# A new order of 880 tasks, with new engines and buffers, for a fused RWKV-5 and MLP-mixer kernel

## The chip, the cores and the metric

The kernel runs on one core of a Trainium2 chip. The metric is the device time of one execution in microseconds (us), the median over several runs. Five engines work side by side, each through its own queue in program order: PE (matrix products; its weight loads, PEld, overlap them), DVE, ACT and POOL (element-wise work), and SP (here only a queue of DMA issues). Sixteen DMA engines move data. Products write to PSUM, 8 banks of 2 KB per partition; DVE and ACT empty the banks.

## The reference, cut to what matters

Inputs r, k, v are (4, 8, 768, 48) in f32: 4 batches, 8 heads, 768 steps, 48 channels. The first half is a linear recurrence over the steps, the second half a mixer block on its output x of (4, 768, 384):

```python
for t in range(S):
    kt, vt, rt = (k[:, :, t], v[:, :, t], r[:, :, t])
    cur = np.einsum('bhd,bhe->bhde', u[None] * kt, vt)
    y[:, :, t] = np.einsum('bhd,bhde->bhe', rt, state + cur)
    state = w[None, :, :, None] * state + np.einsum('bhd,bhe->bhde', kt, vt)
...
xt = x.transpose(0, 2, 1)
h = np.maximum(xt @ w_tok1, 0.0) @ w_tok2       # over the 768 steps, 256 wide inside
u = x + h.transpose(0, 2, 1)
h2 = np.maximum(u @ w_ch1, 0.0) @ w_ch2         # over the 384 channels, 1536 wide inside
return (u + h2).astype(np.float32)
```

## The kernel before, in words

**Tiling.** The 768 steps of a batch are 6 chunks of 128. For a chunk, k and r are multiplied by tables of powers of the decay (on DVE or POOL; tile `kr`, tables `wnat`, `wp`, and `wnpair`, `wpair` where two chunks are loaded as one window `win`), turned so that channels lie on partitions (on PE with a copy out of PSUM into `rka`/`rkb`, or with a DMA transpose into `rk`), and multiplied with each other into scores (`at_ps`). DVE masks the scores into `AT` (kind `mul512p`), PE weighs v by them into `y_ps`, adds what comes from the state, and the result is copied to `x_b`. A step's product with itself (the u term) goes by `pr`, `ad_ps`, `adg`, `yd`. The state `S` is carried from chunk to chunk through `kv_ps`.

The mixer of a batch then makes `h1` from `x_b` and `wtok1` (kinds hid6, or hid3, hid2, hid1 for batch 0, which takes the chunks as they come), goes back over the steps with `wtok2` (kind back), and turns u so that channels lie on partitions: for batch 0 and half of batch 1 on PE (kind turn_x, tile `hx_ps`), for the rest by a DMA transpose `uT<-u_sb` (kind turn_u). Twelve products up (kind up, `z_ps`, three matmuls of 384 columns each) and the products down (kind down, `h_ps`) follow for each half of the batch.

**Whole and half products.** Most matmuls use all 128 rows of the PE array. Those that contract over 64 rows use half of it: scores (kinds scj, sc, sc2: two heads side by side, each on 64 rows), and, for batch 0, whose chunks go in pairs, everything that contracts over the 64 steps of a half window: yv (v weighed), addp2 (own term added), kvp and the second part of kvp_id (state).

**The order.** Nothing in the kernel decides the order when it runs. Every piece of work is a task (a number, an engine, a kind, a function that issues it and its dependences); lists at the head of the file, made by a planner offline, give all the rest:
- `ORDER` (line 21): the sequence in which the 880 tasks are issued. Each engine's queue is what falls to it in this sequence, and the engine keeps to it. So a wait at the head of a queue holds all behind it.
- `BUFS`: for each pool of buffers (`m` are the PSUM banks, 7 of them), which buffer each new tile takes in turn. A task that takes a buffer waits for the last reader of what lay in it.
- `ENGINES`: for each task that can go to either of two or three engines, which one.
- `FILL` (line 139): before which product tasks zero products are issued, and how many. They multiply a tile of zeros and keep PE busy.
- `WAITS`: loads that wait for other loads (not changed).

```python
def run(self):
    done = set()
    for n in self.order:
        emit, deps = self.tasks[n]
        self.now = n
        emit()
        done.add(n)
...
def fill(bank, fresh):
    for i in range(FILL.get(plan.now, 0)):
        pe.matmul(bank, warm[:, 0:128], warm[:, 0:bank.shape[-1]], start=fresh, stop=True, skip_group_check=True)
```

Thirteen more zero products of 512 columns are tasks of their own (867 to 879, kind warm); `FILL[879]` doubles the last.

All instructions issued through these queues have the line number 239 in the profile, so groups are told apart by tile names.

**Task numbers that the text uses.** Batch 0 works on three windows of two chunks. Its tasks:

| what | window 0 | window 1 | window 2 |
|---|---|---|---|
| loads k, r, v (SP) | 51, 52, 53 | 54, 55, 56 | 57, 58, 59 |
| scaled k, two halves | 120, 121 | 149, 150 | 179, 180 |
| scaled r, two halves | 118, 119 | 147, 148 | 177, 178 |
| turned on PE: k, r (tr_all) | 123, 122 | 152, 151 | 182, 181 |
| copied out: k, r | 124, 125 | 153, 154 | 183, 184 |
| product k by r (prod2), summed (sm2), copied (copy_ad) | 126, 127, 128 | 155, 156, 157 | 185, 186, 187 |
| scores, two halves (scj) | 132, 135 | 161, 164 | 191, 194 |
| masks (DVE) | 133, 134, 136, 137 | 162, 163, 165, 166 | 192, 193, 195, 196 |
| v cast; own terms | 129; 130, 131 | 158; 159, 160 | 188; 189, 190 |
| v weighed (yv), own added (addp2) | 138, 139 | 167, 168 | 197, 198 |
| state products, state kept | 140, 143; 141, 144 | 169, 173; 170, 174 | 199; 200 |
| from the state (ys) | 145 | 171, 175 | 201, 203 |

23 is the first product (`w_ps`, the decay spread over partitions), 24 its logarithm (`lnw`), 27 to 30 the four tables (`wnpair`, `wpair`), 8 and 10 the index tables on POOL (`iota_i`), 9 and 11 their casts on DVE. 205, 206, 207 are hid3, hid2, hid1 of batch 0. 111 is the load of `wtok1`, issued by POOL. 518, 547, 576 are the scores of the chunk pairs of batch 2, 698, 727, 756 those of batch 3.

Of the kernel before, what the change touches and what calls it, by code (L numbers as in the profile page):

```python
# [62 lines left out]
    0, 1, 2, 3, 4, 5, 0, 1, 2, 3, 5, 4, 0, 1, 3, 2, 5, 4, 0, 1, 3, 5, 4, 2,  # L63
    ],
# [8 lines left out]
    ],  # L73
    'kp': [
    0, 1, 2, 3, 4, 5, 1, 3, 4, 0, 2, 5, 3, 2, 1, 4, 5, 2, 1, 3, 0, 5, 4, 1, 3, 2, 0,
# [63 lines left out]
FILL = {132: 3, 140: 3, 206: 1, 879: 1}  # L139
# [1116 lines left out]
```

## Time and profile before

| | |
|---|---|
| median of 3 runs | 160.15 us (160.04 to 160.2) |
| profiled execution: span from first to last instruction | 158.2 us |
| profiled execution: its whole time | not given; runs less span: 1.95 us |
| PE busy | 151.8 us (96%) |
| DVE, POOL, ACT busy | 107.0, 90.1, 77.7 us |
| bytes moved by DMA | 27.39 MB, 173 GB/s in the mean |
| granted PE clock, mean | 0.998 |

PE's busy time counts a product from its start to the end of its pipeline, so products that follow closely overlap: a busy PE isn't a PE at its peak. What counts for PE's pace is the distance from one start to the next. In a timeline row the columns are start, length, engine, line, operation, tiles (out<-in), shape and count, and in brackets how long the engine was idle before and what ended that. In a row of windows they are the stretch, its length, and then for each engine its busy time and its number of instructions, the granted PE clock, the mean busy share of the DMA engines (over 1 where transfers overlap) and GB/s. A DMA row on SPq or POOLq shows the issue, not the transfer.

### The profile page before, as it was taken

To read this page: it belongs to the slowest core of one execution; us is meant where nothing else is said; L and a number is where in the kernel's file an instruction comes from. 1 tells how busy PE (TensorE), PEld (TensorE's weight loads), DVE (VectorE), ACT (ScalarE), POOL (GpSimd) and SP (SyncE) were. 2 spreads that over 40 slices of the span, in tenths; PEclk is the share of its full clock that TensorE was granted. 3 is DMA by queue.
4 is the path that set the end of the run, shared out by engine and by line. 5 is a ranking of instruction groups with operands and counts; after the bars stand their busy time and mean duration, and the time that the engine had idled before them with its cause. 6 is when DMAs were issued, how large, how long until landed. Compare 5 with 4: busy or idle time off the path is not lost.

```text
span 158.2 us, 4001 instructions
## 1 busy us (share of the span) xinstructions
PE 151.8 (96%) x1574; PEld 101.3 (64%) x1574; DVE 107.0 (68%) x218; ACT 77.7 (49%) x187; POOL 90.1 (57%) x120
## 2 busy tenths in 40 slices
PE   6988999999999999999999999999999999999991
PEld 1356767776767676666677665576666566666660
DVE  2689992468967994467989637898987465432071
ACT  3677797737990581478476440235643102463000
POOL 7859969444183799999928999398920000000000
PEclk9999999999999999999999999999999999999999
DMA  4999999999989999999999989999992075300044
GB/s 125 265 261 264 205 204 210 229 204 210 227 176 187 203 230 195 187 210 136 220 194 173 227 158 129 190 193 215 145 274 101 29 176 146 126 0 4 0 151 147
DMA packets 88148, 27.39 MB, mean 173 GB/s; under 512 B 82753, under 2 KB 87234, under 8 KB 88130
## 3 DMA queue, kind: packets, MB, share of 16 engines
q1 hardware_dynamic: 85776, 23.86, 76.1%
q0 software_dynamic: 2160, 3.15, 11.7%
q8 instruction: 12, 0.20, 0.5%
q10 hardware_dynamic: 194, 0.14, 0.3%
q14 instruction: 6, 0.05, 0.1%
HBM read 20.65 MB, written 4.72 MB: 160 GB/s over the span
## 4 chain that ended last, share of the span: by engine, by line
PE 87%; DVE 4%; DMA 3%; POOL 2%; ACT 1%; issue 1%; POOLq 0%; ACTq 0%
PE h_ps L239 35%; PE z_ps L239 29%; PE y_ps L239 6%; PE at_ps L239 4%; PE kv_ps L239 3%; PE hT_ps L239 3%; PE hx_ps L239 3%; DVE kr L239 3%; DMA uT<-u_sb 3%; PE tr_ps L239 2%; PE ad_ps L239 1%; PE trk L239 1%; POOL mask L239 1%; ACT rka L239 1%; POOL bm L239 1%
## 5 line engine op out<-in xcount | busy, mean ns | idle before, releaser
L239 PE MATMUL h_ps<-wch,zr 128*128 128x384 bf16 (+2 forms) x300 | 53.4, 319 | 0.0
L239 PE MATMUL z_ps<-uT,wch 128*128 128x384 bf16 x288 | 52.4, 327 | 0.3 <-DMA uT<-u_sb 0.3
L239 ACT ACTIVATE zr<-z_ps 128x384 bf16<-128x384 f32 x63 | 28.7, 492 | 36.1 <-PE z_ps L239 35.9
L239 PEld LDWEIGHTS <-wch 128*128 128x128 bf16 x288 | 31.1, 114 | 13.4 <-DMA uT<-u_sb 0.7
L239 PEld LDWEIGHTS <-zr 128*128 128x128 bf16 x300 | 27.6, 98 | 15.7
L239 DVE TENSOR_TENSOR AT<-at_ps,mask 128x512 bf16<-128x512 f32 x48 | 30.6, 682 | 2.2 <-PE at_ps L239 2.2
L239 DVE TENSOR_SCALAR zr<-z_ps 128x384 bf16<-128x384 f32 x33 | 17.7, 554 | 13.5 <-PE z_ps L239 13.5
L239 POOL TENSOR_TENSOR yd<-vb,adg 128x384 f32<-128x384 bf16 x13 | 10.6, 829 | 10.8 <-ACT vb L239 5.9
L239 DVE TENSOR_TENSOR osb<-u_sb,h_ps 128x384 f32<-128x384 bf16 (+2 forms) x19 | 10.0, 531 | 9.6 <-PE h_ps L239 9.0
L239 PEld LDWEIGHTS <-kr 128*128 128x128 bf16 (+1 forms) x196 | 11.6, 97 | 3.9 <-DVE kr L239 0.7
L239 POOL TENSOR_TENSOR kr<-rt,wp 128x384 bf16<-128x384 f32 x12 | 12.0, 1005 | 3.1 <-DMA rt<-in_r_dram 3.1
L239 POOL TENSOR_TENSOR ku<-kw,u_bc 128x384 f32<-128x384 f32 x12 | 11.9, 1003 | 2.4 <-DMA u_bc<-in_u_dram 2.4
L239 DVE TENSOR_TENSOR u_sb<-x_b,hT_ps 128x384 bf16<-128x384 bf16 x15 | 7.9, 550 | 6.5 <-PE hT_ps L239 6.4
L239 POOL TENSOR_TENSOR rku<-ku,rt 128x384 f32<-128x384 f32 x12 | 12.0, 1002 | 0.2
L239 POOL TENSOR_TENSOR kr<-kw,wnat 128x384 bf16<-128x384 f32 x12 | 12.0, 1004 | 0.0
L239 ACT CAST vb<-vt 128x384 bf16<-128x384 f32 x18 | 9.0, 513 | 2.5 <-DMA vt<-in_v_dram 2.5
L239 PEld LDWEIGHTS <-wtok 128*128 128x128 bf16 x78 | 7.3, 98 | 4.1
L239 DVE TENSOR_TENSOR x_b<-y_ps,yd 128x384 bf16<-128x384 f32 x18 | 9.4, 551 | 0.6 <-PE y_ps L239 0.5
L239 ACT ACTIVATE yd<-vb,adg 128x48 f32<-128x48 bf16 x40 | 9.5, 322 | 0.1
L239 ACT COPY rkb<-tr_ps 128x1024 bf16<-128x1024 bf16 x6 | 6.1, 1013 | 6.7 <-PE tr_ps L239 6.7
L239 PE MATMUL h_ps<-x_b,wtok 128*128 128x384 bf16 x48 | 8.8, 326 | 0.0
L239 PE MATMUL y_ps<-vb,AT 128*128 128x48 bf16 (+1 forms) x240 | 8.4, 182 | 0.0
(99 smaller groups left out, 190.8 us busy)
## 6 DMA issues: line engine op xcount, KB each, us to landing
out_dram<-osb SPq DMA_DIRECT2D x23, 192.0 KB, 2.6
vt<-in_v_dram SPq DMA_DIRECT2D x18, 192.0 KB, 3.5
win<-in_r_dram SPq DMA_DIRECT2D x6, 384.0 KB, 6.2
kw<-in_k_dram SPq DMA_DIRECT2D x12, 192.0 KB, 4.6
rt<-in_r_dram SPq DMA_DIRECT2D x12, 192.0 KB, 4.0
wch<-in_moe_w_ch_dram POOLq DMA_DIRECT2D x4, 384.0 KB, 6.4
win<-in_k_dram SPq DMA_DIRECT2D x3, 384.0 KB, 5.7
win<-in_v_dram SPq DMA_DIRECT2D x3, 384.0 KB, 7.1
```

Source lines behind the costliest of these rows:

```text
L239: return lambda *args, **kw: tc.keep_in_program_order(f(*args, **kw))
```

## The change

Only lists change: `ORDER`, `BUFS`, `ENGINES` and `FILL`. The tasks, their instructions and their dependences stay; each batch computes the same sums.

```diff
 ORDER = [
-    0, 3, 7, 22, 2, 19, 17, 51, 1, 38, 42, 5, 21, 52, 4, 12, 6, 867, 868, 23, 20, 54, 15, 55, 24, 8, 18, 9, 16, 45,
-    27, 58, 29, 120, 28, 13, 43, 118, 30, 53, 14, 121, 10, 149, 57, 869, 870, 871, 872, 873, 874, 875, 876, 877, 878,
...
+    2, 1, 10, 7, 3, 6, 14, 23, 20, 45, 0, 872, 870, 868, 51, 8, 874, 9, 52, 55, 4, 12, 5, 873, 15, 24, 27, 17, 38,
+    878, 19, 42, 54, 13, 58, 876, 53, 30, 41, 18, 21, 22, 120, 28, 29, 25, 26, 121, 123, 869, 16, 11, 118, 124, 119,
...
+    850, 854, 858, 476, 851, 862, 855, 856, 859, 860, 861, 863, 864, 865, 866, 867,
 ]
 BUFS = {
...
 ENGINES = [
-    1, 1, 0, 1, 0, 1, 1, 1, 1, 1, 1, 1, 0, 0, 0, 1, 0, 0, 0, 1, 0, 0, 1, 1, 1, 0, 0, 0, 0, 0, 0, 0, 0, 0, 0, 0, 0, 0,
...
+    0, 1, 0, 1, 1, 1, 0, 1, 1, 1, 1, 1, 0, 0, 1, 0, 0, 0, 0, 0, 0, 0, 1, 1, 1, 1, 0, 0, 0, 0, 0, 0, 0, 0, 1, 0, 0,
...
-FILL = {132: 3, 140: 3, 206: 1, 879: 1}
+FILL = {879: 1}
```

Read out of the lists, engine by engine:

- **FILL.** The zero products before 132 (three of 512 columns), 140 (three of 384) and 206 (one of 384) are gone. The doubled 879 stays.
- **PE, first tasks.** Before: 867, 868, 23, 869 to 878, 123, 879, 122, 25, 44, 152, 132, 135, 127, 151, 140, 181, 161, 143, 156, 164, 182, 169, 138, 194, 145, 139, 167, 173, 175, 171, 191, 168, 186, 199, 205, 197, 201, 198, 203, 206. After: 23, then seven of the warm tasks, 25, 123, one warm, 122, one warm, 44, one warm, 151, 132, 135, 152, 879, 127, one warm, 164, 161, 140, 181, 156, 138, 143, 182, 145, 169, 139, 194, 173, 191, 167, 175, 171, 186, 168, 199, 197, 198, 201, 205, 203, 206. The thirteenth warm task, 867, is the last of all.
- **Changes between whole and half products** along PE's queue: 38 before, 30 after. All eight lie in batch 0; from the scores of batch 1 on, each group of scores still stands alone between whole products, 18 changes in both. Changes among half products between 64 and 128 columns of the array: 3 before, 5 after.
- **DVE, first products.** Before: 120, 118, 121, 149, 119, 147, 148, 126, 134, 136, 133, 141, 155, 128, 162, 144, 137, 166, 163, 165, 185, 195, 196, 174, 192, 193, 190, 204. After: 120, 121, 11, 118, 119, 147, 148, 149, 150, 134, 137, 136, 133, 155, 162, 179, 180, 166, 144, 165, 163, 185, 195, 196, 192, 174, 193, 189, 172, 202.
- **POOL.** Before, the index table 8 stands behind seven other tasks, and 150, 177, 178, 179, 180 are POOL's. After, 8 is fourth (10, 14, 20, 8), POOL has 126, 177 and 178 of the products, and 150, 179, 180 are DVE's; 111 comes after 126, 177, 178, 39, 131 and 130 (before: after 180).
- **Moved between engines in all.** Of the 96 tasks whose kind changes, the most are own terms (POOL 20 to 15, ACT 5 to 9, DVE's products 12 to 15) and copies.
- **SP.** Loads 54 and 55 change places; later loads and stores are interleaved anew. Before the last turn of `rk` for 756, SP has 80 issues before and 82 after; PE's products before 756 add up to 3.3 us less after.
- **The end.** The two halves of the last tile of out change places: 256 columns first, 128 columns last.

More of the change, by code (lines that the diff above doesn't have):

```diff
@@ L62 @@
     'w': [
-    0, 1, 2, 3, 4, 5, 0, 1, 2, 3, 5, 4, 0, 1, 3, 2, 5, 4, 0, 1, 3, 5, 4, 2,
+    0, 1, 2, 3, 4, 5, 0, 1, 2, 3, 5, 4, 0, 1, 3, 2, 5, 4, 0, 1, 5, 2, 3, 0,
     ],
     'm': [
[7 rows of a table removed]
[7 rows of a table added]
     ],
     'kp': [
-    0, 1, 2, 3, 4, 5, 1, 3, 4, 0, 2, 5, 3, 2, 1, 4, 5, 2, 1, 3, 0, 5, 4, 1, 3, 2, 0,
+    0, 1, 2, 3, 4, 5, 1, 2, 4, 0, 3, 5, 1, 4, 0, 2, 1, 3, 0, 5, 4, 1, 2, 0, 5, 3, 4,
     ],
     'p': [
-    0, 1, 2, 3, 4, 5, 0, 2, 0, 3, 1, 4, 2, 0, 5, 3, 1, 4, 2, 0, 5, 3, 4, 1,
+    0, 1, 2, 3, 4, 5, 0, 2, 4, 5, 1, 2, 3, 4, 0, 5, 1, 2, 4, 3, 5, 0, 2, 1,
     ],
     'a': [
-    0, 1, 2, 3, 4, 5, 6, 7, 8, 9, 10, 2, 0, 1, 4, 3, 6, 7, 5, 10, 2, 8, 9, 3, 1, 0, 4, 6, 7, 2, 5, 8, 10, 9, 3, 2, 7,
-    8, 1, 0, 4, 6, 5, 10, 3, 2, 9, 7, 1, 8, 0, 4, 10, 6, 5, 9, 2, 7, 3, 0,
+    0, 1, 2, 3, 4, 5, 6, 7, 8, 9, 10, 0, 1, 2, 3, 4, 5, 6, 7, 0, 8, 9, 10, 1, 3, 2, 5, 7, 4, 8, 9, 0, 6, 10, 1, 3,
+    7, 8, 2, 5, 4, 9, 0, 1, 3, 6, 10, 2, 7, 5, 8, 1, 4, 0, 9, 3, 10, 2, 6, 1,
     ],
     'e': [
-    0, 1, 2, 3, 4, 5, 6, 7, 8, 9, 10, 11, 0, 1, 2, 3, 4, 5, 10, 9, 0, 2, 6, 8, 7, 3, 4, 10, 2, 6, 8, 7, 9, 10, 2, 3,
-    4, 6, 7, 9, 6, 8, 4, 11, 7, 5, 9, 8, 6, 4, 7, 0, 6, 7, 9, 8, 7, 11, 0, 9, 6, 8, 7, 5, 10, 3, 2, 11, 0, 1, 9, 6, 8,
-    7,
+    0, 1, 2, 3, 4, 5, 6, 7, 8, 9, 10, 11, 0, 1, 2, 3, 4, 5, 6, 7, 0, 11, 1, 10, 3, 4, 0, 7, 2, 0, 4, 7, 10, 8, 3, 2,
+    10, 7, 4, 3, 8, 2, 10, 0, 7, 4, 11, 9, 7, 2, 3, 7, 11, 9, 5, 2, 3, 6, 5, 0, 8, 11, 2, 3, 9, 6, 7, 0, 5, 2, 11,
+    4, 9, 1,
     ],
@@ L95 @@
     'l': [
-    0, 1, 2, 3, 4, 5, 6, 7, 8, 9, 10, 11, 0, 2, 1, 3, 4, 5, 6, 7, 8, 9, 10, 11, 1, 3, 5, 6, 0, 8, 9, 2, 4, 7, 10, 11,
+    0, 1, 2, 3, 4, 5, 6, 7, 8, 9, 10, 11, 1, 0, 2, 4, 5, 6, 8, 3, 7, 9, 11, 1, 10, 4, 2, 0, 3, 5, 6, 9, 11, 8, 1, 7,
     ],
     'g': [
-    0, 1, 2, 3, 4, 5, 0, 1, 2, 4, 3, 5, 0, 1, 2, 3, 0, 4, 1, 2, 5,
+    0, 1, 2, 3, 4, 5, 0, 1, 2, 3, 4, 5, 0, 1, 2, 4, 5, 3, 0, 1, 2,
     ],
@@ L104 @@
     'v': [
-    0, 1, 2, 3, 4, 5, 6, 1, 0, 2, 3, 4, 5, 6, 1, 2, 0, 4, 3, 5, 6, 2, 1, 4,
+    0, 1, 2, 3, 4, 5, 6, 0, 1, 2, 3, 4, 5, 6, 0, 1, 2, 3, 4, 0, 5, 1, 6, 3,
     ],
     'u': [
-    0, 1, 2, 3, 4, 5, 6, 7, 1, 0, 2, 5, 4, 3,
+    0, 1, 2, 3, 4, 5, 6, 7, 0, 1, 4, 2, 3, 5,
     ],
     'zr': [
-    0, 1, 2, 1, 0, 2, 1, 0,
+    0, 1, 2, 0, 1, 0, 2, 1,
     ],
```

100 rows, old and new, of tables (BUFS, ENGINES, ORDER) are left out of this document.

## The prediction

> **What bounds the kernel now.** I read the page first: the chain that ended last lies on PE for 87%. The windows then show where that holds.
>
> ```profile
> span 158.2 us, 4001 instructions
> PE 87%; DVE 4%; DMA 3%; POOL 2%; ACT 1%; issue 1%; POOLq 0%; ACTq 0%
> 5.00:12.00 7.00, 6.43 (x69) 3.66 (x71) 5.66 (x10) 5.11 (x10) 4.95 (x13) 1.00 1.27 261
> 12.00:22.00 10.00, 9.27 (x253) 6.68 (x241) 9.97 (x21) 8.01 (x15) 9.20 (x11) 1.00 1.26 227
> 26.00:53.00 27.00, 27.00 (x277) 19.34 (x275) 19.48 (x43) 17.69 (x41) 12.66 (x15) 1.00 1.06 206
> 53.00:116.00 63.00, 62.70 (x643) 42.64 (x641) 48.26 (x97) 31.65 (x87) 54.95 (x59) 1.00 1.07 186
> 154.70:158.20 3.50, 0.00 (x0) 0.00 (x0) 0.42 (x1) 0.00 (x0) 0.00 (x0) 0.90 0.35 117
> ```
>
> From 26 us on PE never rests, but for 0.30 us. Until then it is otherwise: from 12 to 22 us DVE is busy 9.97 of 10 us, more than PE. So a product that goes is worth its full time after 26 us, and before that only as far as DVE lets PE go on.
>
> **The zero products and the changes of shape.**
>
> ```profile
> 9.97 1.01 ACT L239 COPY rkb<-tr_ps 128x1024 bf16<-128x1024 bf16 x1 [0.61 <-PE tr_ps L239]
> 10.86 0.81 PE L239 MATMUL at_ps<-warm 128*128 128x512 bf16 x3
> 11.60 0.64 PE L239 MATMUL at_ps<-rkb,rka 64*64 64x128 bf16 x32
> 12.89 0.35 PE L239 MATMUL ad_ps<-u_blk,pr 128*128 128x8 bf16 x8 [0.65 <-DVE pr L239]
> 13.55 0.65 PE L239 MATMUL kv_ps<-warm 128*128 128x384 bf16 x3
> 14.13 0.51 PE L239 MATMUL kv_ps<-vb,kr 64*128 64x96 bf16 x8
> 24.95 0.33 PE L239 MATMUL h_ps<-warm 128*128 128x384 bf16 x1
> 25.12 0.81 PE L239 MATMUL h_ps<-x_b,wtok 128*128 128x384 bf16 x4
> 68.82 1.14 PE L239 MATMUL z_ps<-uT,wch 128*128 128x384 bf16 x6
> 69.89 0.62 PE L239 MATMUL at_ps<-rk 64*128 64x128 bf16 x16
> ```
>
> Six z products take 1.14 us, the last 0.33 of them its own length, so they start (1.14 - 0.33) / 5 = 0.162 us apart. The next product was due at 68.82 + 6 x 0.162 = 69.79 and starts at 69.89: going from whole to half costs 0.10 us. The way back I take at the same, since the array's arrangement changes there too; its bounds are 0 and 0.10. PE's lists have 38 such changes before and 30 after: 8 x 0.10 = 0.8 us (0.4 if the way back is free), all of it in batch 0.
>
> The zero products took 11.60 - 10.86 = 0.74 us less one change, 14.13 - 13.55 = 0.58 us less one change, and 25.12 - 24.95 = 0.17 us: 0.64 + 0.48 + 0.17 = 1.29 us. The first three cover a wait, for `rkb` ended at 10.98, and 0.65 us after the scores PE waits for DVE all the same; the next three stand in the stretch that DVE fills. Only the last is surely on the path. Together at most 2.1 us; what is left of it is decided by DVE.
>
> **The start, anew.**
>
> ```profile
> 3.90 0.49 ACT L239 ACTIVATE lnw<-w_ps 128x384 f32<-128x384 f32 x1 [0.44 <-PE w_ps L239]
> 4.25 0.21 POOL L239 IOTA iota_i<- 128x2 int32 x2
> 5.08 0.62 ACT L239 ACTIVATE wnpair<-lnw,iota 128x384 f32<-128x384 f32 x1 [0.69 <-DVE u_blk L239]
> 5.73 0.58 DVE L239 TENSOR_TENSOR kr<-win,wnpair 128x384 bf16<-128x384 f32 x1 [0.75 <-ACT wnpair L239]
> 6.63 0.55 DVE L239 TENSOR_TENSOR kr<-win,wpair 128x384 bf16<-128x384 f32 x1
> 10.71 0.99 POOL L239 TENSOR_TENSOR kr<-win,wpair 128x384 bf16<-128x384 f32 x1 [1.64 <-DMA win<-in_r_dram]
> 10.89 1.22 DVE L239 TENSOR_TENSOR kr<-win,wpair 128x384 bf16<-128x384 f32 x1
> 12.14 0.69 DVE L239 TENSOR_TENSOR pr<-tr_ps,rka 128x1024 bf16<-128x1024 bf16 x1
> 16.97 2.48 DVE L239 TENSOR_TENSOR AT<-at_ps,mask 128x512 bf16<-128x512 f32 x4
> ```
>
> The first table (`wnpair`) waits until 5.08 for the index table that POOL makes at 4.25, after seven other tasks. In the new list three short ones stand before it, so that it is ready before `lnw` ends at 4.39; the table can begin at 4.41, and DVE's first product at 5.06: 0.67 us earlier.
>
> From there DVE leads. Masks follow each other at (2.48 - 0.68) / 3 = 0.60 us, products with the tables at about 0.5 us alone. Against the old list DVE loses 126 (the product at 12.14, 0.69 long and so 0.6 like a mask) and 141 (a copy of 384 columns, 0.5), and takes on 150, 179 and 180: 3 x 0.5 = 1.5 us if alone. But the row at 10.89 shows such a product at 1.22 instead of 0.55 us beside POOL's product of the same kind (10.71 to 11.70): it ends 0.41 after POOL's. So the three cost 1.5 to 3.7 us. For the sum I follow the queue: scores at about 9.9 (`rkb` some 1.1 us earlier than at 10.98), four masks from 10.4, prod2 at 12.9, mask 162 at 13.5, then 179 and 180, which wait for the k of window 2, until 15.1 (alone) or 16.7 (each behind a POOL product); then seven steps, 4.1 us in all: 166, 144, 165, 163, 185, 195, 196, where 185 waits for ACT's copies 184 and 183 (to 17.8 in the first case). Mask 196 ends between 19.7 and 20.8.
>
> The Trainium skill, SBUF — State Buffer, section Who interferes with whom, says that a DVE instruction with two inputs in SBUF contends with POOL instructions that read SBUF, and that the later one is blocked until the earlier ends. The row at 10.89 agrees; by this rule alone each of the three products would cost the full 1.2 us and the end of this stretch would be the later of the two.
>
> ```profile
> 15.63 1.03 POOL L239 DMA_DIRECT2D wtok<-in_moe_w_tok_dram  x1
> wtok<-in_moe_w_tok_dram POOLq DMA_DIRECT2D x2, 384.0 KB, 6.3
> 19.32 0.74 PE L239 MATMUL y_ps<-vb,AT 64*128 64x48 bf16 x32
> ```
>
> PE's 167 needs a bank that mask 196 frees, so PE's tail counts from there. In the old list 167 starts at 19.32 and hid2 (206) ends at 25.12 + 4 x 0.162 = 25.77, with nothing idle between: 6.45 us. The new tail from 167 to 206 holds the same tasks without 173 and 191 (0.35 and 0.25, from the rows at 14.13 and 11.60 less the overlap of their last product), without the zero product (0.17), and with five changes of shape for nine (0.4): 6.45 - 0.35 - 0.25 - 0.17 - 0.4 = 5.3 us. So hid2 ends between 19.7 + 5.3 = 25.0 and 26.1, for 25.77 before. **Of everything at the start 0.4 us is left, with bounds -0.3 and 1.2**: not all three products meet one of POOL's, so I stay nearer the early end, and the upper bound holds if the waits for ACT and the banks are shorter than I read them. This holds the zero products and the eight changes already.
>
> One thing is late next: the load of `wtok1` (111), issued at 15.63 by POOL now and landing 6.3 us later. POOL's new list puts it behind 126 (two halves of about 1.15), 177, 178, 39, 131 and 130, which I place at 16.7; it lands at 23.0, and hid3 asks for it at 23. Cost 0 to 0.5; I take 0, and keep the 0.5 in the range.
>
> **The middle.** Work on PE is the same from there. The old list has one stall left:
>
> ```profile
> 97.06 0.49 PE L239 MATMUL hT_ps<-h1r,wtok 128*128 128x384 bf16 x2
> 98.17 1.29 SPq L239 DMA_TRANSPOSE uT<-u_sb  x1
> 101.52 0.66 PE L239 MATMUL z_ps<-uT,wch 128*128 128x384 bf16 x3
> 102.47 0.84 PE L239 MATMUL z_ps<-uT,wch 128*128 128x384 bf16 x4 [0.30 <-DMA uT<-u_sb]
> ```
>
> Three z products from 101.52 end their turn at 102.01; the next starts at 102.47: 0.46 us lost. From the end of the last hT product's turn (97.38) to that start are 5.1 us, for DVE's sum, SP's issue and the transfer. In PE's new list 5.2 us of products stand between the same two tasks (4.6 before), and 5.5 and 7.6 us for two of the others; for the first turn of batch 3 it is 4.2 (4.9 before), in a stretch where few transfers run. I take 0.35 of the 0.46 as won; bounds -0.3 and 0.46.
>
> **The end.**
>
> ```profile
> 154.36 0.79 DVE L239 TENSOR_TENSOR osb<-u_sb,h_ps 128x128 f32<-128x128 bf16 x2 [0.40 <-PE h_ps L239]
> 155.18 0.38 ACTq L239 DMA_DIRECT2D out_dram<-osb  x1
> ```
>
> After PE's last product come a sum of 256 columns and its store, until 158.2. After the change the 128-column half is last: half the bytes and a shorter sum. I take 0.1 us, bounds 0 and 0.4. The zero product 867, now after the last real product, has these 3.5 us as cover; without them it would cost 0.2 us.
>
> **The sum.** 0.4 + 0.35 + 0.1 = 0.85 us off the span: 157.35 us. The page gives no whole time for its execution; the runs' median stands 160.15 - 158.2 = 1.95 us above the span, which I leave as it is: 159.3 us.
>
> **The rivals.**
>
> *All of it counts (157.9 us).* If PE and not DVE sets the pace from 10 us on, the scores start 1.1 us earlier (9.9 for 11.05, when `rkb` would have let them), 0.8 us of changes and 0.65 us of zero products go, and 0.35 + 0.1 follow as above: less the share counted twice in the waits (0.7), 2.3 us. For it speaks PE at 9.27 of 10 us; against it DVE's 9.97. Behind this: the Trainium skill, TensorEngine Tiling (Array Packing), section Key Properties, says that a change of tiling mode drains PE; by that the changes among half products count too, 41 before and 35 after, and this rival would be 0.2 us slower. No row above parts the two.
>
> *Nothing is left (160.1 us).* The products 150, 179 and 180 each wait for POOL, `wtok1` is late, and another turn takes the place of the one at 102.47: 0 at the start, 0.1 at the end.
>
> *Slower (161.6 us): the last scores wait for their turned keys.*
>
> ```profile
> 109.03 4.66 SPq L239 DMA_TRANSPOSE rk<-kr  x2
> 115.59 0.62 PE L239 MATMUL at_ps<-rk 64*128 64x128 bf16 x16
> SPq L239 <- POOL rku L239: 10.6, 7, 2.7
> ```
>
> PE asks for 756 at 115.59 now; the last turn's issue ends at 113.69. In the new list 3.3 us less of products stand before 756, so with the 0.75 us won by then it is asked for at 111.5. SP has two issues more before that turn. If SP and POOL keep their pace, the turn comes at 113.69 + 2 x 0.7 plus some 2 us of transfer, 5 us too late. Against it: POOL has five products of 1 us fewer before the keys of 756, and SP waited 10.6 us for POOL, which that shortens. It decides from the point where these gain less than 5 us together; a loss of half, 2.4 us, less the 0.85 won, gives 161.7, say 161.6.
>
> *The clock comes late (160.2 us).*
>
> ```profile
> 3.80 4.06 PE L239 MATMUL kv_ps<-warm 128*128 128x512 bf16 x10
> 8.14 0.59 PE L239 MATMUL kv_ps<-warm 128*128 128x512 bf16 x2
> ```
>
> The first ten zero products take 4.06 / 10 = 0.41 us each; later, two last 0.59 (at 8.14) and three 0.81 us (at 10.86), so that one more costs only 0.22: PE runs at half pace for about the first 7.5 us, though the granted clock reads 1.00. Its work began at 1.25 us; in the new list it begins with the spread product at 2.22. If the full pace comes 1 us later for it, turns and scores until 8.5 us take twice as long: 0.5 us, and more if single zero products between the turns don't keep it busy: up to 0.9 us, all of the gain and a little. Behind this: the Trainium skill, TensorE: Matmul & The Clock Gate, Part 1, says that the pace rises after a window of about 3.4 us of sustained work, free-running; by that it could come up to 3.4 us later, and this rival's time would be 160.4 us as an estimate.
>
> *The change doesn't do what it says:* not so for the zero products and the 38 to 30, which are counted in the lists; that they lie where PE waits anyway is the rival of 160.1.
>
> **How the numbers follow.** Forecast 159.3 us (its own range 158.7 to 159.8): 0.45. All of it, 157.9: 0.14. Nothing, 160.1: 0.17. Slower, 161.6: 0.17. Clock, 160.2: 0.07. The range reaches from the middle of the fast rival to most of the slow one: 157.9 to 161.3. What a measurement of this kernel can tell from no change is 0.2%, 0.3 us. Faster: 0.41 of the forecast, 0.14, and 0.02 of the others: 0.57. Same: 0.04 + 0.12 + 0.03 = 0.19. Slower: 0.17 + 0.03 + 0.04 = 0.24.
>
> **What would show it.** Right: DVE's first table product near 5.1; no `warm` into `at_ps` or `h_ps`; DVE at 9.9 of 10 us from 12 to 22, with products of 1.0 us or more beside POOL's; hid2 ending up to 1.2 us earlier; no idle PE before z products for `uT`. Wrong: PE ahead by 1.5 us at 26 us (DVE didn't lead); PE idle before `at_ps` for `rk` near 104 or 111 (the slow rival); zero products 0.41 us apart after 8 us (the clock); stalls for banks between 26 and 120 us, which I have put at nothing because the covers in PE's list are as long as before.

## The result and the profile after

The changed kernel takes 172.98 us in the median (170.99 to 175.07), the kernel before 160.18 us beside it: a ratio of 1.071, with a 95% interval of 1.067 to 1.075. The ratios here and below leave out executions that lie more than 1.5% above the fastest of the same kernel (here 175.07 us and the profiled one), so that this one is below the ratio of the medians (1.080). The forecast was 159.3 us and the range ended at 161.3. The profiled execution took 173.89 us, of which 172.2 are its span; the account below is of this one execution.

From the page of the changed kernel: span, the chain that ended last by engine, and the granted clock in 40 slices.

```profile
span 172.2 us, 4013 instructions
PE 54%; DMA 17%; DVE 10%; POOL 6%; issue 6%; SPq 4%; ACT 3%; POOLq 0%; DVEq 0%
PEclk9999999999995699999999999999999999999999
```

The chain lay on PE for 87% before, and for 54% now: PE waits. The windows of the same execution (columns as before) show where.

```profile
12.00:22.00 10.00, 8.39 (x225) 6.38 (x226) 9.81 (x17) 7.72 (x16) 9.94 (x12) 1.00 1.12 207
26.00:53.00 27.00, 22.21 (x235) 15.83 (x233) 20.61 (x35) 15.28 (x39) 13.77 (x16) 0.99 1.11 210
53.00:116.00 63.00, 58.54 (x548) 38.41 (x548) 44.23 (x89) 30.90 (x95) 41.95 (x44) 0.95 0.91 157
53.00:60.00 7.00, 6.42 (x45) 3.72 (x45) 4.13 (x9) 1.91 (x8) 1.00 (x1) 0.56 1.05 186
```

From 26 to 53 us PE rests 27.00 - 22.21 = 4.79 us (0 before), from 53 to 116 it rests 4.46 us (0.30 before), and from 53 to 60 us it runs at 0.56 of its clock, which is worth 7 x 0.44 = 3.1 us more by this estimate. These three are 12.1 of the 14.0 us between the two spans. The rest is at the start (0.9 us from 12 to 22, 0.9 from 22 to 26) and behind 116 us (1.0), less a remainder of some 0.8 us, which the zero products and changes of shape that are gone can account for; no run prices them apart.

The longest waits of PE after its first product in this execution: us in total, times, the longest.

```profile
PE h_ps L240 <- DVE AT L240: 3.4, 1, 3.4
PE z_ps L240 <- DMA uT<-u_sb: 2.4, 1, 2.4
PE at_ps L240 <- DMA rk<-kr: 2.2, 3, 1.1
```

The longest is a down product (281) that waits for a mask of DVE's to free its bank. The timeline shows the start of the kernel first and then what that mask waited for.

```profile
5.04 0.63 DVE L240 TENSOR_TENSOR kr<-win,wnpair 128x384 bf16<-128x384 f32 x1 [0.71 <-ACT wnpair L240]
10.25 0.64 PE L240 MATMUL at_ps<-rkb,rka 64*64 64x128 bf16 x32
22.09 1.63 DVE L240 TENSOR_TENSOR ydb<-vb,adg 128x384 bf16<-128x384 bf16 x1
23.78 0.50 PE L240 MATMUL y_ps<-ydb,place 64*128 64x384 bf16 x4 [0.94 <-DVE ydb L240]
25.54 0.81 PE L240 MATMUL h_ps<-x_b,wtok 128*128 128x384 bf16 x4
...
47.42 0.59 POOL L240 DMA_DIRECT2D wch<-in_moe_w_ch_dram  x1
48.04 0.84 POOL L240 TENSOR_TENSOR yd<-vb,adg 128x384 f32<-128x384 bf16 x1
48.33 4.60 DVE L240 TENSOR_TENSOR kr<-kt,wnat 128x384 bf16<-128x384 f32 x1
48.83 0.83 POOL L240 TENSOR_TENSOR wGm<-bm,wG 128x384 f32<-128x384 f32 x1
49.62 0.99 POOL L240 TENSOR_TENSOR kr<-kt,wnat 128x384 bf16<-128x384 f32 x1
50.57 1.94 POOL L240 TENSOR_TENSOR kr<-kw,wnat 128x384 bf16<-128x384 f32 x2
52.85 0.68 DVE L240 TENSOR_TENSOR AT<-at_ps,mask 128x512 bf16<-128x512 f32 x1
53.58 1.44 PE L240 MATMUL h_ps<-wch,zr 128*128 128x384 bf16 x4 [3.38 <-DVE AT L240]
```

A product of keys on DVE (task 377, at 48.33), 0.55 us long when alone, took 4.60 us. POOL went from product to product until 50.57 + 1.94 = 52.51; 377 ended 0.42 us later, at 52.93. The mask stood behind it in DVE's queue, and PE behind the mask. 377 was DVE's task before as well; only its place in the order changed.

### The profile page after: what moved, and what is told of

It reads as the page before. It is cut to its first block, busy times and chain, and to the rows that moved or that the text cites. A ratio compares the mean times of both kernels' runs of the same rounds, so it can differ in the third digit from the quotient of the medians.

```text
span 172.2 us, 4013 instructions
## 1 busy us (share of the span) xinstructions
PE 154.1 (89%) x1567; PEld 102.6 (60%) x1567; DVE 115.5 (67%) x226; ACT 83.2 (48%) x219; POOL 85.4 (50%) x111
## 4 chain that ended last, share of the span: by engine, by line
PE 54%; DMA 17%; DVE 10%; POOL 6%; issue 6%; SPq 4%; ACT 3%; POOLq 0%; DVEq 0%
PE h_ps L240 27%; PE z_ps L240 14%; DMA kt<-in_k_dram 5%; DVE AT L240 4%; DMA rk<-kr 4%; SPq L240 4%; PE y_ps L240 3%; PE kv_ps L240 3%; DMA vt<-in_v_dram 3%; POOL rku L240 2%; DMA rt<-in_r_dram 2%; PE at_ps L240 2%; POOL kr L240 2%; DVE kr L240 2%; DMA out_dram<-osb 2%
## 5 line engine op out<-in xcount | busy, mean ns | idle before, releaser
L240 PE MATMUL h_ps<-wch,zr 128*128 128x384 bf16 (+2 forms) x300 | 56.2, 330 | 3.4 <-DVE AT L240 3.4
L240 PE MATMUL z_ps<-uT,wch 128*128 128x384 bf16 x288 | 53.0, 327 | 2.5 <-DMA uT<-u_sb 2.4
L240 PEld LDWEIGHTS <-zr 128*128 128x128 bf16 x300 | 28.5, 100 | 20.6 <-issue 5.5
L240 DVE TENSOR_SCALAR zr<-z_ps 128x384 bf16<-128x384 f32 x34 | 18.4, 554 | 15.9 <-PE z_ps L240 15.9
L240 ACT ACTIVATE yd<-vb,adg 128x48 f32<-128x48 bf16 x72 | 17.0, 321 | 10.1 <-DVE adg L240 10.0
L240 PEld LDWEIGHTS <-kr 128*128 128x128 bf16 (+1 forms) x196 | 12.4, 99 | 7.0 <-issue 2.6
L240 POOL TENSOR_TENSOR yd<-vb,adg 128x384 f32<-128x384 bf16 x8 | 6.7, 834 | 15.9 <-DVE adg L240 7.5
L240 POOL TENSOR_TENSOR pr<-rka,rkb 128x512 bf16<-128x512 bf16 x4 | 5.0, 1257 | 7.9 <-ACT rkb L240 3.4
```

Source lines behind the costliest of these rows:

```text
L240: return lambda *args, **kw: tc.keep_in_program_order(f(*args, **kw))
```

## The experiments

### The product 377 on the other engine

```diff
 ENGINES, entry 122 (task 377)
-    1   (DVE)
+    0   (POOL)
```

> The changed kernel with one product, task 377 (a window of keys by its table), on POOL instead of DVE; nothing else differs. In the changed kernel this product took 4.60 us on DVE (48.33 to 52.93) while POOL ran without a pause until 52.51, and a mask stood behind it that frees PE's bank. Theory one (this wait and the slow clock after it are a loss of their own, and the later waits for keys and loads another): PE starts its down product 281 at about 50.1 instead of 53.58, the granted clock stays at 1.00 and the four groups of down products take 0.65 instead of 1.28 us; 3.5 + 2.9 us less, 172 - 6.4 = 165.6 us, between 164 and 167.5. Theory two (all that comes later follows from this stall, since ACT's and POOL's lists wait for PE's products): the waits at 105 to 118 us go as well, 161 us or less. Rival (from 60 us on the loads and POOL set the end): PE comes earlier and waits longer for turned keys, 170 to 173 us.

168.84 us, a ratio of 1.049 (1.043 to 1.055) against 1.071 (1.067 to 1.075). The time lies between the range of theory one and that of the rival. Windows of the profiled execution:

```profile
53.00:60.00 7.00, 7.00 (x92) 4.89 (x91) 5.82 (x13) 5.43 (x17) 4.08 (x6) 1.00 0.95 200
100.00:116.00 16.00, 12.50 (x93) 7.34 (x90) 7.80 (x16) 5.45 (x16) 10.30 (x11) 0.89 1.07 183
```

Between the starts of the tasks 362 and 298 PE needs 7.8 us (52.09 to 59.93) instead of 14.1 (49.87 to 63.95): 6.2 us less, for 6.4 expected by theory one. The median gained 4.1 us (3.5 by the two ratios, 0.022 x 160.2), and in the profiled execution PE waited longer for the keys of 343 (2.4 us at 40 to 43 for 2.0, and a clock of 0.72 from 40 to 46 for 1.00). The waits from 100 to 116 us are as long as before (3.5 us) and have moved forward with PE: theory two falls.

### The clock

```diff
-FILL = {879: 1}
+FILL = {879: 1, 362: 20}
```

> The changed kernel with 20 zero products of 384 columns (3.25 us) before the products of task 362, which stands ahead of PE's idle 3.55 us; the result is the same, as they add zero. If the idle time is what brings the clock down, the four groups of down products behind it take 0.65 us each instead of 1.28 and the granted clock of 53 to 60 us reads 1.00 instead of 0.56: 2.9 us less at 59 us, 169 to 170 us at the end if that is kept, 172 to 173 if the later waits for keys take it back. If the clock falls for another reason than idleness, the down products stay at 1.28 us and the time at 172 to 174.

172.58 us (1.065 to 1.077): no gain in the whole, but the timeline shows the stretch as expected.

```profile
51.26 3.51 DVE L240 TENSOR_TENSOR kr<-kt,wnat 128x384 bf16<-128x384 f32 x1
52.80 3.41 PE L240 MATMUL kv_ps<-warm 128*128 128x384 bf16 x20
57.09 2.11 PE L240 MATMUL h_ps<-wch,zr 128*128 128x384 bf16 x12
```

With PE kept busy, twelve down products take 2.11 us, 0.16 us each; in the changed kernel four of them are 1.44 us long, 0.32 each. In the changed kernel the clock reads 0.50 from 53 to 59 us. So there the clock fell with the idle time, and that cost about as much again as the wait was long. It doesn't have to: in the changed kernel with the zero products put back (below) PE waits as long for the same mask, and runs at full pace behind it (clock 1.00 from 53 to 60 us).

```profile
55.86 0.81 PE L240 MATMUL h_ps<-wch,zr 128*128 128x384 bf16 x4 [3.37 <-DVE AT L240]
```

Each of these is one execution, so the filled one alone doesn't show that idleness decides. In it PE had waited 2.5 us at 40 to 43 us instead, and the clock fell there (0.87 in 40 to 53 us).

```diff
-FILL = {132: 3, 140: 3, 206: 1, 879: 1}
+FILL = {879: 1}
```

(in the kernel before, nothing else)

> The kernel before with the seven inner zero products (three at 132, three at 140, one at 206) gone and nothing else changed. The prediction's reading (DVE leads until 22 us and the first six are hidden): between nothing and 0.2 us, 159.9 to 160.2 us. Rival (PE leads and all of 1.29 us counts): 158.9 us. A second rival (they keep the clock up in the waits that they fill): slower, 160.5 us or more.

161.08 us, a ratio of 1.005 (1.002 to 1.008): slower, in the range of the second rival. The windows are of the longest execution, 163.86 us; they show where time can go, not how often it does.

```profile
12.00:22.00 10.00, 9.04 (x153) 7.05 (x155) 9.02 (x19) 5.53 (x9) 9.26 (x11) 0.57 1.27 228
```

0.57 from 12 to 22 us, against 1.00 with the zero products. Over a whole execution the clock has a mean of 0.968 to 0.979 in four of the twelve (162.30 to 163.86 us), and of 0.995 or more in the 17 of the kernel before. So the zero products keep the clock in some executions. In the other eight of the twelve the mean is 0.996 or more, and they still take 160.64 to 161.29 us, for a median of 160.37 before: what makes this half microsecond is not shown. Put back into the changed kernel, at the same three tasks, the zero products don't help:

> The changed kernel with the seven inner zero products put back (three at 132, three at 140, one at 206). With them gone from the kernel before, PE ran 12 to 22 us at a granted clock of 0.57 in one execution, and the median was 0.5% longer. If they keep the clock up in the changed kernel too: 0.5 to 1.5 us less, 171.5 to 172.5 us, and DVE's or PE's tail at the start not later. If DVE leads there and the clock is full anyway: 0 to 0.3 us more, 173 to 173.5.

174.55 us (1.074 to 1.090), longer than both expectations. The clock was at 1.00 there without them in the first place, and in this execution PE rested longer from 22 to 26 us (1.55 us for 0.94).

### What holds 377

> No kernel of the problem: only single instructions, and the output is not computed. POOL runs n products of two SBUF tiles in a row (n = 0, 1, 2, 4, 7, about 1 us each), and DVE, released at the same moment, runs one copy and then one product of two SBUF tiles; then the same with a DMA issue between POOL's second and third product, with a DVE product of two bf16 tiles, a DVE copy of one tile, a DVE product of a PSUM and an SBUF tile, and one POOL product beside a run of DVE's. Theory (DVE gets in only when POOL pauses): DVE's product ends 0.4 us after POOL's last one, so it takes about 0.55, 1, 2, 4 and 7 us; with a copy or a PSUM tile 0.55 to 0.7 us. Rival (it waits for the one POOL instruction that is running): never over 1.4 us, whatever n.

The product took 0.55 us for n = 0 and 1.35 us for n = 1, 2, 4 and 7, with the issue between as well (there it had ended before POOL came to the issue): the rival, and the theory falls in this form. A copy of one SBUF tile, 0.36 us alone, took 1.03 to 1.15 us; the product of a PSUM tile stayed at 0.55.

> Single instructions again, no output of the problem. In the first set DVE's product of two SBUF tiles came in after the first of POOL's products whatever their number (1.35 us for n = 1, 2, 4, 7), though task 377 took 4.60 us beside five of them and ended 0.42 us after the last. So here POOL runs five, with one thing of the kernel's each time: results written in rows of 48 with gaps on POOL's side, on DVE's, on both; a product of PSUM ahead of DVE's; POOL's results read by another engine; and all of it with two products by a column first. Theory (the form decides): one of these takes 4 us or more, the plain one 1.35. Rival (the moment decides, not the form): all take 1.0 to 1.6 us, and the cause of the 4.60 us stays open.

0.55 to 1.35 us in all seven; the form decides nothing. But in each changed kernel so far in which 377 stayed on DVE it waited to the end of POOL's run: 4.60 us (run ends at 52.51, 377 at 52.93), 3.51 (54.35, 54.77), 4.58 (54.78, 55.20), and 2.50 with a shorter run, of the kernel of the next section (with 384 on ACT):

```profile
48.61 0.59 POOL L231 DMA_DIRECT2D wch<-in_moe_w_ch_dram  x1
50.67 2.50 DVE L231 TENSOR_TENSOR kr<-kt,wnat 128x384 bf16<-128x384 f32 x1
51.76 0.99 POOL L231 TENSOR_TENSOR kr<-kw,wnat 128x384 bf16<-128x384 f32 x1
```

What these share is POOL's DMA issue ahead of the run. In the changed kernel with 117 (that issue) moved ahead of 355:

> The changed kernel with POOL's DMA issue of the weights 117 ahead of 355 (at about 43 us) instead of right in front of the run of products beside which DVE's product 377 waits (47.4 to 48.0 us). In four executions 377 took 2.50 to 4.60 us and each time ended 0.42 us after POOL's last product, while the same forms alone let DVE in after one product (0.81 to 1.35 us). Theory (the issue in front makes the difference): 377 takes 0.8 to 1.4 us. Rival (something else in this place does): 3 us or more, and it ends 0.42 us after POOL's last one again.

377 took 0.55 us, and the one execution 170.0 us. But POOL happened to stand still when 377 came, so this alone doesn't decide it. The single instructions do:

> Single instructions, no output of the problem. DVE runs some products of PSUM first, so that its product of two SBUF tiles comes in the middle of POOL's run: in the second of six products; the same with a table that POOL reads too; behind a DMA issue of POOL's with five products after it; beside 14 copies of ACT's; before two products by a column; and all of that together as around task 377. Theory A (whoever comes in the middle of a run waits to its end): 3.5 us or more in all six. Theory B (the DMA issue in front makes it): only in the third and the last. Rival: 1.0 to 1.6 us in all, and the cause stays open.

POOL and DVE in two of the six, one execution; the first pair is the plain run of products, the other stands behind a DMA issue.

```profile
7.27 5.12 POOL L37 TENSOR_TENSOR o_mid<-pa,pb 128x384 bf16<-128x384 f32 x5
8.09 0.60 DVE L37 TENSOR_TENSOR e_mid<-ta,tb 128x384 bf16<-128x384 f32 x1
22.54 0.93 POOL L37 DMA_DIRECT2D wide<-in_moe_w_ch_dram  x1
23.49 4.79 POOL L37 TENSOR_TENSOR o_dmafirst<-pa,pb 128x384 bf16<-128x384 f32 x5
23.90 4.80 DVE L37 TENSOR_TENSOR e_dmafirst<-ta,tb 128x384 bf16<-128x384 f32 x1
```

0.60 us in the middle of a plain run, and 4.80 us behind the issue: it ended at 28.70, POOL at 28.28, 0.42 earlier, as in the kernel. With all things together it took 1.02 us, which theory B doesn't give.

> Single instructions, no output of the problem. POOL: one product, a DMA issue, and then: five products with DVE's product coming in the first (keys1) or the third (keys3); two products (one); one product by a column and four products (yd1); two by a column and three products (yd2); five beside ACT's copies (act); two products, one that waits for ACT, and four more in which DVE's comes (gate). Theory (behind an issue POOL keeps its way to SBUF from product to product until it pauses): keys1 4.8, keys3 about 3, one about 1.9, yd1 and yd2 4 us or more, act 4.8, gate 1.4 or less. Rival (the product right behind the issue decides, and a product by a column lets DVE in): yd1 and yd2 about 1, the others as above.

Of these, DVE in the third product behind the issue, beside two products, beside two by a column, and behind a pause of POOL's:

```profile
16.89 4.80 POOL L37 TENSOR_TENSOR o_keys<-pa,pb 128x384 bf16<-128x384 f32 x5
19.27 2.83 DVE L37 TENSOR_TENSOR e_keys<-ta,tb 128x384 bf16<-128x384 f32 x1
25.62 1.95 POOL L37 TENSOR_TENSOR o_one<-pa,pb 128x384 bf16<-128x384 f32 x2
26.15 1.85 DVE L37 TENSOR_TENSOR e_one<-ta,tb 128x384 bf16<-128x384 f32 x1
40.07 2.00 POOL L37 TENSOR_TENSOR o_yd<-vb,pb 128x384 f32<-128x384 bf16 x2
40.60 0.78 DVE L37 TENSOR_TENSOR e_yd<-ta,tb 128x384 bf16<-128x384 f32 x1
61.59 4.16 POOL L37 TENSOR_TENSOR o_gate<-pa,pb 128x384 bf16<-128x384 f32 x4
61.68 1.32 DVE L37 TENSOR_TENSOR e_gate<-ta,tb 128x384 bf16<-128x384 f32 x1
```

keys1 4.59, act 4.68, yd1 4.52 us. So behind a DMA issue POOL's run of products keeps DVE's product out until POOL pauses (2.83 us are what was left of the run, and 0.4 us); without the issue, or after a pause, DVE gets in between two products. One exception stays unexplained: two products by a column in a row let it in (0.78 us, and 1.02 above). Why an issue does this is not shown either.

### POOL's lead, the loads, SP's list

```diff
 ENGINES, entry 127 (task 384)
-    0   (POOL)
+    2   (ACT)
```

> The changed kernel with task 384 (a row's own value, a product by one column) on ACT as it was before, instead of POOL; nothing else differs. POOL stood still for 6.92 us ahead of this product (56.22 to 63.14, it waits for sums that PE makes late), with all of batch 2's key products behind it. Theory (the lead that POOL loses there makes the turned keys late, and PE waits for them at 91, 107, 112 and 119 us, 4.5 us in all): these waits go, 172 - 4.5 = 167.5 us, 166.5 to 169. Rival (SP's queue, with stores and turns in another order, makes them late): 171 to 174, with the waits still there.

> Both products back on the engines that the other list gives them time on: 377 on POOL and 384 on ACT. If the two causes are separate their gains add: 168.8 (with 377 alone) - 4.5 = 164.3 us, 163 to 165.5; what is left over the kernel before is then the wait for the keys of 345 and 341 at 40 to 44 us and the slow clock behind it (4 us) and the start. If the later waits come from SP's queue: 168 to 169.5. If POOL, with one product more at 49 us, is late by itself: over 169.

171.87 us (1.054 to 1.068) and 170.44 us (1.054 to 1.065). POOL's stand of 6.92 us shrank to 2.92, and PE still waited 2.4 us for the turned rows and 2.3 for the keys. The second is not faster than 377 alone. The theory of POOL's lead falls.

The loads of keys on SP and DVE's products with them, first before and then after the change:

```profile
13.49 5.51 SPq L239 DMA_DIRECT2D kt<-in_k_dram  x3
34.84 0.55 DVE L239 TENSOR_TENSOR kr<-kt,wnat 128x384 bf16<-128x384 f32 x1
38.51 0.62 DVE L239 TENSOR_TENSOR kr<-kt,wnat 128x384 bf16<-128x384 f32 x1
```

```profile
13.49 4.12 SPq L240 DMA_DIRECT2D kt<-in_k_dram  x2
28.96 4.78 SPq L240 DMA_DIRECT2D kt<-in_k_dram  x3
39.41 0.56 DVE L240 TENSOR_TENSOR kr<-kt,wnat 128x384 bf16<-128x384 f32 x1 [1.97 <-DMA kt<-in_k_dram]
```

Three loads of keys went out before SP stood for the first weights, now two; the third, 70, goes out at 28.96, ahead of those that PE needs at 40 us. Moved back, with 377 on POOL:

```diff
 ORDER
-    63 ... 62, 66, 70, 65
+    63, 70 ... 62, 66, 65
```

(SP's tasks alone; two entries of `BUFS` change places with it)

> The changed kernel with 377 on POOL and one load of keys, task 70, issued on SP ahead of the stand for the first weights (behind 63, as before) instead of behind it (28.96 us). Theory (with one load more behind the stand, the keys of 343 and 351 land at 40 to 43 us, while the kernel before had them by 38.5; PE waits 1.9 to 3.6 us for them at 40 to 44 us and then runs at half pace for some 3 us): the wait goes, 168.8 - 2 to 4.5 = 164.5 to 167 us. Rival (the load competes with the weights, which come later then, and PE waits at 23 to 30 us instead): 168 to 170. Rival two (the later waits for keys take back what is won): 168 to 169 with longer waits at 103 to 109 us.

167.58 us, 1.046 (1.044 to 1.049). In this execution PE waits 1.6 us at 40 to 42 (2.4 without the move), and the clock reads 1.00 from 12 us on. The gain is 1.3 us by the medians and 0.4 us by the ratios, less than the theory's 2 to 4.5; the interval overlaps that of 377 alone (1.043 to 1.055), so it is not shown.

```diff
 ORDER
-    423 ... 416, 498
+    423, 416 ... 498
```

> The same, and one turn on SP, task 416, issued right behind 423 (at about 77 us, as before) instead of at 93.6 us, where SP stands 3.45 us for it with the loads of batch 3's r behind it, for which POOL waits 3.3 us, for whose keys PE waits at 107 us and for whose turn SP keeps the turn 603, for which PE waits at 112 us. Theory (this one turn in SP's list makes the waits at 103 to 112 us, some 3.5 us, and the slow clock after them): 3 to 4.5 us less than with load 70 alone. Rival (SP's list is late as a whole there, by loads, stores and turns in their new order): 0 to 1 us less. A third way: the turn waits for a buffer there and holds SP up earlier: slower.

168.30 us (1.045 to 1.055). Windows of the kernel with load 70, and then windows and one row of the timeline with turn 416 as well:

```profile
100.00:116.00 16.00, 12.05 (x102) 7.86 (x103) 8.77 (x17) 7.57 (x21) 10.56 (x12) 1.00 1.16 215
```

```profile
22.00:26.00 4.00, 4.00 (x89) 2.80 (x83) 3.23 (x6) 1.90 (x5) 2.02 (x3) 0.50 1.15 175
100.00:116.00 16.00, 15.03 (x123) 9.50 (x122) 11.36 (x23) 7.42 (x22) 10.56 (x12) 1.00 1.10 202
```

```profile
83.53 0.40 PE L195 MATMUL at_ps<-rk 64*128 64x128 bf16 x8 [1.88 <-DMA rk<-kr]
```

The waits from 100 to 116 us fall from 3.95 to 0.97 us, but that 416 set them isn't shown: PE has lost the time before. Keys are late at 83.53 (1.88 us), the clock is at 0.57 from 84 to 88 us, and PE asks for the scores 4.3 us later than with load 70 alone (104.23 for 99.94), while SP begins the turns of keys ahead of them only 1.5 us later (95.79 for 94.28). In this execution the clock was at 0.50 from 22 to 26 us as well. Nothing is left in the whole.

The six stores of batch 0 forward in SP's list (285 and 290 behind 81, 280 and 300 behind 93, 295 and 305 behind 423), alone and with the three other edits:

> The changed kernel with the six stores of batch 0 moved forward in SP's list (285 and 290 behind load 81, 280 and 300 behind load 93, 295 and 305 behind turn 423) and nothing else changed. Theory (the late stores hold buffers that POOL's products wait for, 5.2 us, and make the keys late): POOL's waits for stores go, and of PE's waits at 91 to 119 us (4.5 us) half or more: 169.5 to 171.5 us. Rival (the loads of batch 3's r and k and the turn 416 in front of them set these waits): 172 to 174, with the waits in place though POOL no longer waits for stores.

> 377 on POOL, load 70 and turn 416 early, and the six stores of batch 0 early. Theory (these four account for most of what was lost): against 168.3 us with the first three, the waits at 114 us (0.84) and part of 83 us (1.88) go: 165.5 to 167.5 us. Rival (each move on SP puts another load later, so the wait wanders): 167.5 to 169.5, with a new wait between 75 and 120 us.

170.80 us (1.054 to 1.068; single times 169.19 to 174.64) and 169.76 us (1.046 to 1.062). Alone the median is 2.2 us lower, with overlapping intervals, and in the profiled execution PE waits as long for keys (2.3 us for 2.2) and 1.6 us for rows (2.4 before); together nothing is gained, POOL still waits 5.8 us for a store, and PE waits 1.54 us at 80.55 and 1.64 at 82.59. The rival holds: the wait wanders.

### Order or engines, and a faster version

The kernel before with the changed list `ENGINES`:

> The kernel before, its order of work, buffers and zero products, with the changed kernel's list of engines (which of ACT, DVE and POOL makes each copy, product and relu) and nothing else of the change. Theory (the order carries the loss, as waits for engines and loads that come later): 160 to 162 us. Rival (the choice of engines carries it): 164 us or more.

169.23 us, 1.057 (1.053 to 1.062): the theory falls. What PE waited for there:

```profile
PE ad_ps L239 <- POOL pr L239: 2.1, 2, 1.3
PE h_ps L239 <- ACT zr L239: 1.6, 1, 1.6
PE y_ps L239 <- ACT osb L239: 1.2, 1, 1.2
```

These are other waits than those of the changed kernel, so this doesn't share the loss out between order and engines: the new list of engines doesn't fit the old order, and costs nearly as much there as the whole change. The other half, the new order with the old engines, was not run.

Two tries for a version faster than both, on the kernel before:

> The kernel before with two tasks moved: the index table that the first table waits for (8) comes first on POOL, and the second product of the first window's r (119) stands ahead of 149 on DVE, so that it is done before POOL's product 150 begins. Theory (these two things of the change's start are a gain without the rest: the first scores start 0.6 us earlier or more): 159.5 to 160.0 against 160.4 to 160.9 of the kernel before in these runs, so a ratio of 0.994 to 0.997. Rival (DVE leads from 12 us on and takes it back): the ratio is 0.999 to 1.002.

> The kernel before with one task of PE's list moved: the first z product of the second half of batch 2 (628), which waits 0.3 to 0.5 us for its turned rows at 102.47, three z products later, and its relu with it. If the wait is filled and nothing else moves: 0.3 to 0.46 us less, a ratio of 0.997 to 0.998. If the relus behind it come later and take it back: 0.999 to 1.002.

1.000 (0.998 to 1.002) both. DVE's first product came at 5.07 instead of 5.73 us and the first scores at 11.23 instead of 11.60, and by 19.3 us PE was where it had been (167 starts at 19.34, 19.32 before): the lead was gone inside the stretch that DVE fills (9.72 of 10 us from 12 to 22). With 628 later, the wait of 0.3 us is gone and one of 0.6 us for a relu on DVE stands at 106.4. No version here beats the kernel before.

## Why the prediction was wrong, step by step

- **The start.** DVE led, as read: 9.81 of 10 us from 12 to 22. Its first product came at 5.04 (5.06 forecast), the first scores at 10.25 (9.9), mask 196 ended at about 20.5 (19.7 to 20.8). But hid2 ended at 25.54 + 0.65 = 26.19, for 25.0 to 26.1 forecast and 25.77 before: 0.4 us lost instead of 0.4 won. The tail from 167 took 6.3 us and not 5.3. The term left out is the own product 189, which the change gave to DVE: 1.63 us beside POOL's 190 and an issue (22.09), for which PE waited 0.94.
- **The zero products.** The prediction had most of them hidden and none of them useful. Taken out alone they make the kernel before 0.5% slower; in four executions of twelve the clock falls with them gone, and the rest is open. The row from 12 to 22 us with a clock of 1.00 rested in part on these products, and I read it as given.
- **The changes of shape** (0.8 us) were in the sum for PE, and DVE led; no run tells their price apart.
- **Three products beside POOL's, 1.5 to 3.7 us.** These three stayed near the early end: 150 took about 0.5 us (9.85 to 10.88 for 149 and 150), 179 and 180 took 1.66 together at 14.79. But the bound took the wait for one POOL product as the worst, and the row at 48.33 shows a wait for a whole run. This is the mechanism that the prediction missed, and it hit a product that it had not looked at, 377, since its engine didn't change.
- **The middle: "stalls for banks ..., which I have put at nothing because the covers in PE's list are as long as before".** This is the step that failed. The covers are counted in PE's products, and what they must cover had changed: DVE's queue ahead of the mask (3.38 us of wait and 3.1 us of clock, 6.2 by moving 377), keys that come late at 40 to 43 us (2.0 us here; with load 70 moved forward the keys of 343 are there 0.6 us earlier), and from 91 us on keys and turned rows (some 4.5 us; that SP's new order makes them late is argued, not shown). The 0.35 us to be won at 102.47 became a wait of 2.39 us for the same kind of transfer at 112.00.
- **The load of `wtok1`**, landing at 23.0 forecast, landed at 24.07 and hid3 began at 24.39 without a wait for it: right at nothing, by luck. PE had just lost the 0.94 us to 189; without them hid3 would have stood ready at 24.39 - 0.94 = 23.45 by this estimate, ahead of the load, and in the kernel with the three edits and the stores PE did wait 0.95 us for it (at 25.13). **The end**: from PE's last product of the problem to the end of the span 3.2 us, 3.5 before: 0.3 won, inside the bounds.
- **The rivals.** The slower one had the kind right, keys that come late through SP and POOL, and its place wrong: 756 didn't wait, scores at 91, 107 and 119 us did. It had one wait of 2.4 us where there were eight. The clock's rival looked at the first 10 us only; there the pace rose in time (eight turns in 0.85 us at 7.39, in 0.61 at 8.29).
- **The range** added the bounds of the terms that I had named. None stood for a list made anew having more waits than the one left in the old list.

**What stays open.** With 377 and load 70 mended the kernel is 7.3 us over the one before. In that execution PE rests 8.0 us between 12 and 150 us (1.0 before), half of it from 100 to 116. Which of SP's tasks are too late I could not show: after each move of one, others came late. No single cause of the rest was found.

## What to carry to other kernels

When a whole order is made anew, don't count the covers in the bound engine's list alone: for each wait that it hides, follow the queue of the engine that it waits for, and ask what that queue's head waits for (here a product of two SBUF tiles beside POOL). Ask of each filler whether it keeps the clock, before it is called free to take out. And don't take over a list of engines without the order that it was made for: on the old order it cost 9 us here.

## What the runs showed of the hardware that I had not expected

- **POOL's run behind a DMA issue shuts DVE out.** A product of two SBUF tiles, 0.55 us alone, takes 0.55 to 1.35 us beside POOL's products, but 1.85 us beside two, 2.83 beside the rest of five and 4.6 to 4.8 beside five, if POOL has issued a DMA just ahead and doesn't pause (two products by a column in a row are the exception, 0.78 to 1.02). The Trainium skill, SBUF — State Buffer, section SBUF: two separate sides, has the shared way to SBUF locked for one instruction; that agrees with the plain runs (1.35 us), and the runs behind an issue differ: there the measurement decides.
- **A wait can cost more than its length.** With 3.38 us of idle time at 53.58 PE came to half pace for the next 5 us; with 3.37 us at 55.86, in the changed kernel with the zero products, it didn't (clock 1.00). 2.39 us at 112.00 did not (clock 1.00), 2.52 us at 107.98 in the kernel with 377 on POOL did (0.89 in 100 to 116). The Trainium skill, TensorE: Matmul & The Clock Gate, Part 1, has a window of about 3.4 us that runs freely, so that the moment of a wait counts beside its length; these rows agree in that. The 2.52 us that were enough are shorter than such a window, so a wait below its length is not safe either.
- **Repeated runs spread.** The changed kernel lies between 170.99 and 175.07 us, the kernel before between 160.04 and 160.45 beside it. In the profiles of the changed kernels the waits for loads and the clock differ from one to the next; how much of the spread each makes is not shown.
